# A transformer layer with compressive-memory attention and an MLP on one Trainium2 core: an opening written out in program order, first layer norms through ScalarE and a PSUM bank of their own, b2 added to the stored residual, late row blocks and first MLP weights placed anew

## The chip, the cores and the metric

One core of one Trainium2 chip runs the whole program. TensorE multiplies matrices into eight PSUM banks of 128 x 512 float32; VectorE (DVE), ScalarE (ACT) and GpSimd (POOL) do the elementwise work; SyncE (SP) issues most of the DMAs, in the order of its queue, and ScalarE issues some. Each engine runs its own instructions in order and waits for the others through semaphores. The metric is the device time of one execution in microseconds (us), lower is better; a kernel is timed in several runs, of which the median is given.

## The reference

S = 2048 rows of D = 1024, 32 heads of 32, four segments of 512 rows, and an MLP of width F = 3584, everything in float32:

```python
y = layernorm(x)
q, k, v = y @ wq, y @ wk, y @ wv
...
for s in range(4):
    a_dot = softmax(q_s k_s.T * 32 ** -0.5 + causal_mask) @ v_s
    a_mem = (phi(q_s) @ M) / (phi(q_s) @ z + 1e-6)
    o_s = g * a_mem + (1 - g) * a_dot
    M, z = M + phi(k_s).T @ v_s, z + sum(phi(k_s))
h = x + o @ wo
y2 = layernorm(layernorm(h))
out = h + gelu(y2 @ w1 + b1) @ w2 + b2
```

Here phi(t) is t + 1 above zero and exp(t) below, and g = sigmoid(beta), one number per head.

## The kernel before

*Numbers as two halves.* Every product of full precision is made of three fast ones: an operand is split into an upper half `h` (a rounded copy, on ACT or VectorE) and a lower half `l` (the operand minus `h`, on VectorE or POOL), and TensorE adds h·h, h·l and l·h into one bank (`mm3`, L110). `split` (L87) makes the two halves of a weight block, and `load_block` (L193) loads a 128-column block into one of the two `wr` buffers of the pool `wp` and splits it into `wh` and `wl` (three of each).

*Stages.* The rows are worked on in two halves of 1024, each of two segments of 512 (`sl` 0 and 1) or eight row blocks of 128.

- 0 to 22 us: the opening. The identity, the gates from beta and the transposed b1 are made (L53 to L75), and `ln1(0, 0)` (L181) normalises the first segment: it loads four row blocks `xt`, and for each `ln_scale` (L115) makes mean and scale (statistics on VectorE, the power on POOL), `ln_tiles` (L139) normalises, and `ln_transpose` (L127) transposes on TensorE into `pt`, copies the upper half on ACT (`yh`) and subtracts the lower half on VectorE (`yl`). In this one call the normalisation is an ACT instruction with scale and offset, the offset `nb` being made on VectorE.
- 22 to 575 us, and 930 to 1480 us for the second half: `attention`. `dense` makes q, k and v of four heads and one segment; each such unit is interleaved with the slots of the heads of the unit before. The first unit has no heads yet and is interleaved with `ln1(half, 1)`, the second segment's layer norm, instead.
- 530 to 648 and 1480 to 1558 us: `wo_seg`, the output projection. `finish` and its `fold` transpose a column block back and add it to the residual tiles `hts`. While the second segment goes through, `ln2` (L583) stores the first segment's finished residual to `h1_dram` (`store_h`, L579), normalises it in place and transposes it.
- 648 to 732 and 1558 to 1642 us: `Mixer.lead`, the first of the products of `w1`. The MLP's two multiplications are made by a Strassen scheme, that is by seven products of sums and differences of quarters instead of eight. `load`, `upper` and `lower` bring column blocks of `w1` (tiles `wx`, `wh`, `wl`). Beside it `ln2_combined` (L590) stores and normalises the second segment and forms the scheme's operands (`fold`, with tiles such as `b12t`).
- 732 to 930 and 1642 to 1841 us: `Mixer.pair`, twenty steps for one pair of column blocks, some 13.6 us each: products into `bps` and `dps`, GELU on ACT, results to `h_dram` in DRAM. Under the last nine pairs of the first half `ln1(1, 0, 2)` runs, a step of it for every 0.15 steps of the pairs.
- 1841 to 2393 us: `Second`, the product with `w2`, in 2 x 7 combinations of seven row blocks each (KP = 7). `load_rows` (L870) loads the rows of `w2` of one row block into a tile `w2r`, one of four buffers tagged "ln" in `lnp`; `fill` (L881) forms the combination (POOL), splits it (`hi` on ACT, `lo` on VectorE) and, for combinations 7 and 6, stores the sum to `t_dram` for later use, which holds the buffer until the store is done. `load_items` (L908) loads the rows of the hidden activations `hr` that the left operands are made of. `out` (L968) loads the stored residual into the tile `c`, to which `add` adds every product, and `bias` (L991) adds b2 to it in 32 steps after the eighth to the 43rd product. `fills` has a due time for every row block; `rows_ahead` (L902) loads as far ahead as four buffers allow, the b2 tile counted as one. Before the stage starts, `fill_at` (L1128) lists the places in the last pairs at which the first fourteen row blocks are filled; two of its combinations (q 0 and 1) have to be there when the stage starts.

*What sets the order.* Within `in_order()` (L98) each engine runs what is traced in program order; `lead`, the pairs and `Second` are traced inside it. Elsewhere, in the opening, the attention and the output projections, the scheduler of the language chooses the order from dependences; `queue_after` (L94) adds a single order between two instructions.

*PSUM.* Three banks have the tag "d" (`ps_dense`), two "qk", two "pt" and one "av". The transposes `pt` of the layer norms share the three "d" banks with `kps`, `qps`, `vps`, `pwo`, `pn`, `bps` and `dps`. The one "av" bank holds the attention's `po` of 64 partitions.

Of the kernel before, what the change touches and what calls it, by code (L numbers as in the profile page):

```python
# [16 lines left out]
P = 128  # L17
S = 2048
D = 1024
H = 32  # L20
# [22 lines left out]
def build(tc, x, wq, wk, wv, wo, beta, w1, b1, w2, b2, out):  # L43
# [20 lines left out]
    nc.sync.dma_start(bb, bass.AP(tensor=beta.tensor, offset=beta.offset, ap=[[0, P], [1, H]]))  # L64
    nc.scalar.activation(bb, bb, AF.Exp, scale=-1.0)
    nc.vector.tensor_scalar(bb, bb, 1.0, None, op0=ALU.add)
    nc.vector.reciprocal(gate[:, 0, :], bb)
    nc.vector.tensor_scalar(gate[:, 1, :], gate[:, 0, :], -1.0, 1.0, op0=ALU.mult, op1=ALU.add)

    b1r = const.tile([FB, P], F32, name="b1r")  # L70
    nc.sync.dma_start(b1r, b1.rearrange("(f p) -> f p", p=P))
    b1c = const.tile([P, FB], F32, name="b1c")
    pb = ps_dense("pb")
    nc.tensor.transpose(pb[:, :FB], b1r, ident[:FB, :FB])
    nc.vector.tensor_copy(b1c, pb[:, :FB])  # L75
# [11 lines left out]
    def split(pool, w, hi, lo, hi_eng="vector", lo_eng="gpsimd"):  # L87
        if hi_eng == "vector":
            acts["hi"] = nc.vector.tensor_copy(hi, w)
        else:  # L90
            acts["hi"] = nc.scalar.copy(hi, w)  # L91
        return getattr(nc, lo_eng).tensor_tensor(lo, w, raw(hi), op=ALU.subtract)  # L92

    def queue_after(late, early):  # L94
        tc.add_manual_dep(late.ins, early.ins.name, NOSYNC, reason="issue order")

    @contextmanager
    def in_order():  # L98
# [6 lines left out]
        for ins in traced[n:]:  # L105
            if ins.engine in last:
                tc.add_manual_dep(ins, last[ins.engine].name, NOSYNC, reason="program order")
            last[ins.engine] = ins

# [5 lines left out]
    def ln_scale(pool, src, double):  # L115
        st = pool.tile([P, 2, 6], F32, name="st", bufs=3)
        for i in range(2):
            nc.vector.bn_stats(st[:, i, :], src[:, 512 * i:512 * i + 512])
# [5 lines left out]
        acts["pow"] = nc.gpsimd.tensor_tensor(v[:, 1:2], v[:, 0:1], mhalf, op=ALU.pow)  # L124
        return mv[:, 0:1], v[:, 1:2]

    def ln_transpose(pool, src, xh, xl, t4):  # L127
        for c in range(2):
            pt = ps_dense("pt").rearrange("p (a b) -> p a b", a=4)
            for i in range(4):  # L130
# [6 lines left out]
                                    op=ALU.subtract)  # L137

    def ln_tiles(pool, tiles, xh, xl, double, gap=1, act=False, fold=None):  # L139
        fold = fold or (lambda src, t4: ln_transpose(pool, src, xh, xl, t4))  # L140
        for t in range(5):
            if t < 4:
                m, r = ln_scale(pool, tiles[t], double)
                for _ in range(gap):
                    yield
                if act:
                    nb = pool.tile([P, 1], F32, name="nb", bufs=4)
                    nc.vector.scalar_tensor_tensor(nb, m, -1.0, r, op0=ALU.mult, op1=ALU.mult)
# [32 lines left out]
    def ln1(half, sl, delay=0):  # L181
# [9 lines left out]
        yield from ln_tiles(lnp, xs, yh, yl, False, act=(half == 0 and sl == 0))  # L191

    def load_block(pool, w, c0, wbufs, hi_eng="vector", lo_eng="gpsimd"):  # L193
# [4 lines left out]
        acts["split"] = split(pool, wr, wh, wl, hi_eng, lo_eng)  # L198
        return wh, wl

    def attention(half):
# [3 lines left out]
        nc.gpsimd.memset(mask, 0.0)  # L205
# [4 lines left out]
        if half == 0:  # L210
            nc.gpsimd.memset(mz_flat, 0.0)
# [225 lines left out]
        def av(st, n):  # L437
            u, j = st["u"], st["j"]
            if n == 0:
                st["po"] = psum.tile([64, 512], F32, tag="av", name="po", bufs=1)  # L440
# [49 lines left out]
        def weights(g):  # L490
            ws = {}
            for n, w in (("k", wk), ("q", wq), ("v", wv)):
                ws[n] = load_block(wp, w, g * P, 3, "vector" if g or n == "k" else "scalar")
                if g == 0 and n != "k":
                    queue_after(acts["split"], acts["pow"])
            return ws

        ws = weights(0)
# [84 lines left out]
    def ln2(half, sl, hts):  # L583
# [3 lines left out]
        store_h(half, sl, hts)  # L587
        yield from ln_tiles(lnp, hts, zh, zl, True, 2)

    def ln2_combined(half, hts, zx):  # L590
# [9 lines left out]
        store_h(half, 1, hts)  # L600
# [44 lines left out]
        yield from ln_tiles(lnp, hts, None, None, True, 2, fold=fold)  # L645
# [533 lines left out]
```

## Time and profile before

| what | value |
| --- | --- |
| median of three runs | 2394.14 us (2392.71 to 2401.14) |
| profiled execution, its own time | 2394.96 us |
| span of its instructions | 2393.2 us |
| TensorE's mean granted clock | 0.993 |
| data moved by DMA | 356.95 MB, mean 149 GB/s |

How to read its lines: engines are PE (TensorE), DVE, ACT, POOL and SP, and L656 is line 656 of the kernel. In a timeline a row is start, duration, engine, line, operation, out<-in with shapes and, in brackets, how long the engine had stood idle and what released it. In the list of waits a row is the waiting instruction, what released it, total us, number of waits and the longest. In the groups, "x32 | 39.3, 1229 | 0.0" is 32 instructions, 39.3 us in all, 1229 ns each, and no idle time ahead of them. In the chain of waits a row is a step's start and duration. A window gives PE, PEld (weight loads), DVE, ACT and POOL busy time, with the number of instructions, then the granted clock, the share of the DMA engines and GB/s.

### The profile page before, as it was taken

Reading aid. Unit: us, or ns where it says so; the run is one execution under the profiler, and the core shown is the slowest. Engines: PE = TensorE matmul, PEld = TensorE weight load, DVE = VectorE, ACT = ScalarE, POOL = GpSimd, SP = SyncE. Lnnn points to the kernel's source line nnn. Section 1 sums busy time; section 2 is a strip of 40 time slices with the busy share of each in tenths; the row PEclk is TensorE's granted clock in tenths of the full one; section 3 lists DMA queues with packets and bytes.
Section 4 is the critical chain, followed back from the end, with each engine's and each line's share of the span. In section 5 each row is a group of like instructions: output and inputs, shape, how many; then the busy total and the mean of one; then the engine's idle time right before and its main releaser. Section 6 shows DMA issues by size and latency. Waiting matters only on the chain.

```text
span 2393.2 us, 35708 instructions
## 1 busy us (share of the span) xinstructions
PE 2308.3 (96%) x11873; PEld 1906.4 (80%) x11873; DVE 1628.4 (68%) x3470; ACT 1212.0 (51%) x2557; POOL 1065.5 (45%) x1011
## 2 busy tenths in 40 slices
PE   6999999999999989999999999999998989999999
PEld 5888888877787878888888877777886878888887
DVE  6777777775475664777777776466565888667763
ACT  4677676775363333677777776254343223232321
POOL 3444444444164442455555544245443554245430
PEclk9999999999999999999999999999999999999999
DMA  5333333333466654433333334366566976476762
GB/s 170 91 89 88 82 84 85 89 105 120 145 207 201 186 151 131 122 85 85 85 86 84 88 95 126 128 211 195 157 187 212 328 258 213 153 251 227 250 222 96
DMA packets 348161, 356.95 MB, mean 149 GB/s; under 512 B 26286, under 2 KB 251594, under 8 KB 347978
## 3 DMA queue, kind: packets, MB, share of 16 engines
q1 hardware_dynamic: 284810, 317.98, 44.3%
q10 hardware_dynamic: 63168, 36.71, 5.2%
q8 instruction: 94, 1.54, 0.3%
q14 instruction: 89, 0.73, 0.1%
HBM read 227.11 MB, written 77.14 MB: 127 GB/s over the span
## 4 chain that ended last, share of the span: by engine, by line
PE 72%; DVE 9%; ACT 6%; DMA 6%; issue 3%; POOL 3%; SPq 1%; ACTq 0%; DVEq 0%; POOLq 0%
PE po L1031 21%; PE bps L656 7%; PE ppt L428 5%; PE dps L656 5%; PE po L448 5%; PE pqk L396 3%; PE kps L111 2%; PE kps L112 2%; PE kps L113 2%; PE vps L111 2%; PE vps L112 2%; PE vps L113 2%; PE pwo L113 2%; PE pwo L111 2%; PE pwo L112 2%
## 5 line engine op out<-in xcount | busy, mean ns | idle before, releaser
L412 POOL TENSOR_SCALAR pr<-pr,nm,gate 128x128 f32<-128x128 f32 (+3 forms) x512 | 322.2, 639 | 409.0 <-DVE nm L409 307.3
L405 ACT ACTIVATE pr<-pr,mx 128x256 f32<-128x256 f32 (+3 forms) x512 | 287.8, 562 | 175.8 <-DVE mx L397 171.3
L397 DVE CUSTOM_DVE_ANT_0 pr<-pqk,mask 128x256 f32<-128x256 f32 (+3 forms) x512 | 243.4, 483 | 38.4 <-PE pqk L396 35.3
L435 DVE TENSOR_TENSOR ptl<-ppt,pth 128x512 fp32r<-128x512 f32 (+1 forms) x384 | 227.2, 597 | 53.5 <-ACT pth L430 51.4
L428 PE MATMUL ppt<-ident,pr 128*128 128x128 f32 x1280 | 222.7, 277 | 1.9 <-DVE ptl L435 1.8
L430 ACT CAST pth<-ppt 128x512 fp32r<-128x512 f32 (+1 forms) x384 | 194.1, 518 | 51.5 <-PE ppt L428 46.5
L92 POOL TENSOR_TENSOR wl<-wr,wh 128x1024 fp32r<-128x1024 f32 x64 | 152.9, 2390 | 103.2 <-ACT wh L91 48.4
L428 PEld LDWEIGHTS ppt<-ident,pr 128*128 128x128 f32 x1280 | 164.0, 140 | 32.1 <-DVE ptl L435 3.6
L1041 DVE TENSOR_TENSOR c<-c,po 128x512 f32<-128x512 f32 x160 | 105.2, 682 | 116.2 <-PE po L1031 115.8
L396 PE MATMUL pqk<-ks,qs 96*128 96x256 f32 (+3 forms) x512 | 162.7, 318 | 1.3 <-DVE mx L397 1.3
L448 PE MATMUL po<-ptl,vs 128*64 128x512 f32 (+3 forms) x512 | 154.2, 311 | 5.8 <-DVE ptl L435 5.6
L448 PE MATMUL po<-pth,vs 128*64 128x512 f32 (+3 forms) x512 | 155.5, 326 | 1.3 <-ACT pth L430 1.1
L888 POOL TENSOR_TENSOR w2r<-w2r 128x512 f32<-128x512 f32 x56 | 90.2, 1622 | 83.9 <-DMA w2r<-in_B_w 70.9
L1031 PE MATMUL po<-w2h,zh 128*128 128x512 f32 x378 | 122.2, 393 | 3.8 <-DVE zh L960 3.3
L409 DVE RECIPROCAL nm<-mx 128x2 f32<-128x2 f32 x256 | 42.2, 165 | 112.6 <-ACT pr L405 112.2
L396 PEld LDWEIGHTS pqk<-ks,qs 96*128 96x128 f32 x512 | 96.0, 188 | 26.4 <-DVE mx L397 6.3
L1031 PE MATMUL po<-w2h,hl 128*128 128x512 f32 x322 | 104.1, 393 | 6.4 <-DVE c L1041 6.4
L111 PE MATMUL vps<-yh,wh 128*128 128x512 f32 x256 | 109.0, 426 | 0.2 <-ACT omt L378 0.2
L111 PE MATMUL kps<-yh,wh 128*128 128x512 f32 x256 | 108.3, 423 | 0.0
L111 PE MATMUL qps<-yh,wh 128*128 128x512 f32 x256 | 107.2, 419 | 0.0
L111 PE MATMUL pwo<-oh,wh 128*128 128x512 f32 x256 | 104.8, 411 | 0.6 <-ACT oh L91 0.6
L113 PE MATMUL pwo<-oh,wl 128*128 128x512 f32 x256 | 101.5, 397 | 0.0
(233 smaller groups left out, 6751.5 us busy)
## 6 DMA issues: line engine op xcount, KB each, us to landing
hr<-h_dram SPq DMA_DIRECT2D x112, 448.0 KB, 5.0
w2r<-in_B_w SPq DMA_DIRECT2D x126, 256.0 KB, 3.9
r<-in_B_w SPq DMA_DIRECT2D x56, 512.0 KB, 4.5
h_dram<-ht ACTq DMA_DIRECT2D x84, 256.0 KB, 3.7
ks<-kh SPq DMA_DIRECT2D x256, 64.0 KB, 2.0
qs<-qh SPq DMA_DIRECT2D x256, 64.0 KB, 2.0
wr<-in_A_wo SPq DMA_DIRECT2D x32, 512.0 KB, 4.4
wx<-in_B_w SPq DMA_DIRECT2D x56, 256.0 KB, 3.6
```

The costliest lines, as they stand in the source:

```text
L111: nc.tensor.matmul(ps, ah, bh, start=first, stop=False)
L113: nc.tensor.matmul(ps, al, bh, start=False, stop=last)
L396: nc.tensor.matmul(pqk[:, :n], u["qs"][j][:, i * P:(i + 1) * P], u["ks"][j][:, 0:n], start=True, stop=True)
L397: nc.vector.tensor_tensor_reduce(out=st["pr"][:, offs[i]:offs[i] + n], in0=pqk[:, :n], in1=mask[:, 512 - n:512], op0=ALU.add, op1=ALU.min, ...
L405: nc.scalar.activation(pi, pi, AF.Exp, bias=mx[:, i:i + 1], scale=-1.0, accum_out=mx[:, 4 + i:5 + i])
L412: nc.gpsimd.tensor_scalar(pi, pi, nm[:, 4 + k:5 + k], gate[:, 1, 4 * g + j:4 * g + j + 1], op0=ALU.mult, op1=ALU.mult)
L428: nc.tensor.transpose(ppt[:, o:o + P], pr[:, offs[i] + jk * P:offs[i] + (jk + 1) * P], ident)
L430: nc.scalar.copy(pth[:, base:base + w], ppt[:, :w])
L435: nc.vector.tensor_tensor(o, x0, x1, op=ALU.subtract)
L448: nc.tensor.matmul(po[:, P * jk:], v, st[part][:, koff[jk]:koff[jk] + w], start=(jk, part) == (0, "pth"), stop=(jk, part) == (2, "ptl"))
L656: nc.tensor.matmul(ps, x_[:, c, :], y_[:, c, :], start=first and c == 0 and n == 0, stop=last and c == 3 and n == 2, skip_group_check=True)
L1031: nc.tensor.matmul(ps, x_[:, k], y_[k], start=opens and k == 0 and i == 0, stop=closes and k == self.KP - 1 and i == 2, skip_group_check=True)
```

## The change

- *Opening.* `opening()` takes the place of `ln1(0, 0)` and of the first `weights(0)`: all inside `in_order()`. SP loads the four blocks of x first, then the first blocks of wk and wq, then beta and b1 (the instructions on these are now in `constants()`, called late). Row blocks 0 and 3 are normalised on ACT, 1 and 2 on POOL; `nb` is made on POOL. The halves of wk, wq and wv are split at fixed places. `behind` puts the statistics of the following layer norm and three memsets of `attention` after the opening on their engines.
- *First layer norms.* `ln1` transposes into the "av" bank (`po` becomes the lower 64 partitions of a full tile) with one more step between its transposes, and normalises on ACT in every call (`act=True`), `nb` on POOL (`ln_offset`). Its rate beside the first unit of a half goes from 0.5 to 1.1 steps per step, and under the pairs from 0.15 to 0.16.
- *b2.* `ln2` loads b2 into a tile of the pool `pp`. For every row block, `residual` adds it on POOL into `hb` (two buffers) right after the block's statistics and stores `hb` instead of the tile itself. `store_h` and `Second.bias` are removed, and with them the b2 tile in the ring of four.
- *Late row blocks.* Row blocks 4 and 5 of combination 1 are loaded into the `wr` buffers of `wp` (`APART`), and the last eight places of `fill_at` are moved.
- *First MLP weights.* The loads of w1's blocks -1 and 0 and the split of -1 move from `lead` into `begin`, called at the 57th step of the second `wo_seg`.

```diff
+    def constants():
+        nc.scalar.activation(bb, bb, AF.Exp, scale=-1.0)
...
+    def behind(op):
+        tc.add_manual_dep(op.ins, acts["last"][op.ins.engine].name, NOSYNC, reason="program order")
...
-            nc.vector.bn_stats(st[:, i, :], src[:, 512 * i:512 * i + 512])
+            op = nc.vector.bn_stats(st[:, i, :], src[:, 512 * i:512 * i + 512])
+            if "last" in acts:
+                behind(op)
...
+    def ln_offset(pool, m, r):
+        nb = pool.tile([P, 1], F32, name="nb", bufs=4)
+        nc.gpsimd.tensor_scalar(nb, m, -1.0, r, op0=ALU.mult, op1=ALU.mult)
+        return nb
...
-            pt = ps_dense("pt").rearrange("p (a b) -> p a b", a=4)
+            pt = (take or ps_dense)("pt").rearrange("p (a b) -> p a b", a=4)
...
+            if take:
+                yield
...
+                if act:
+                    nb = ln_offset(pool, m, r)
+                if aside:
+                    aside(t)
...
-                    nb = pool.tile([P, 1], F32, name="nb", bufs=4)
-                    nc.vector.scalar_tensor_tensor(nb, m, -1.0, r, op0=ALU.mult, op1=ALU.mult)
...
-        yield from ln_tiles(lnp, xs, yh, yl, False, act=(half == 0 and sl == 0))
+        def take(name):
+            return psum.tile([P, 512], F32, tag="av", name=name, bufs=1)
+
+        yield from ln_tiles(lnp, xs, yh, yl, False, act=True,
+                            fold=lambda src, t4: ln_transpose(lnp, src, yh, yl, t4, take))
+
+    def opening():
...
+        with in_order():
+            scale(0)
+            scale(1)
+            normal(0)
+            normal(1)
+            scale(2)
+            normal(2)
+            turn(0)
+            lower(0, 0)
+            scale(3)
+            turn(1)
+            halves("k", "vector")
+            lower(1, 0)
+            turn(2)
+            normal(3)
+            lower(2, 0)
+            turn(3)
+            lower(3, 0)
+            lower(3, 1)
+            halves("q", "scalar")
+            load("v", wv)
+            constants()
+            halves("v", "scalar")
+        return ws
...
-                    interleave(d, ln1(half, 1), 0.5)
+                    interleave(d, ln1(half, 1), 1.1)
...
-    def store_h(half, sl, hts):
-        for t in range(4):
-            nc.sync.dma_start(h1_dram[half * NT + 4 * sl + t], hts[t])
...
+        def aside(t):
+            hb = pp.tile([P, D], F32, name="hb", bufs=2)
+            nc.gpsimd.tensor_tensor(hb, hts[t], b2c, op=ALU.add)
+            nc.sync.dma_start(h1_dram[half * NT + 4 * sl + t], hb)
...
+            load(-1)
+            load(0)
+            upper(-1)
+            lower(-1)
+            self.early = load, upper, lower, left
...
+        APART = ((1, 4), (1, 5))
...
+            if (q, k) in self.APART:
+                t = wp.tile([P, DC, P], F32, tag="wr", name="w2s", bufs=2).rearrange("p a b -> p (a b)")
...
-                    len(self.rows) + (self.b2c is not None) < 4:
+                    (len(self.rows) - sum(r in self.rows for r in self.APART) < 4):
...
-            if n > 6 and self.b2c is not None and n % 16 < 14:
-                t, c = self.unbiased.pop(0)
-                o = self.out(t, c)
-                nc.vector.tensor_tensor(o, o, self.b2c[:, c * 512:(c + 1) * 512], op=ALU.add)
...
-        interleave(wo_seg(half, 1, hts1, pp, iter(()), evac), ln2(half, 0, hts), 0.5)
+        interleave(hooked(wo_seg(half, 1, hts1, pp, iter(()), evac), lambda k: mixer.begin(), 57, 1),
+                   ln2(half, 0, hts, pp), 0.5)
...
-            interleave(chain(*(mixer.pair(j) for j in range(HP - 9, HP))), ln1(1, 0, 2), 0.15)
+            interleave(chain(*(mixer.pair(j) for j in range(HP - 9, HP))), ln1(1, 0, 2), 0.16)
...
-            fill_at = [(j, 5) for j in range(HP - 8, HP - 2)] + [(HP - 3, 13), (HP - 2, 12), (HP - 2, 14), (HP - 1, 0),
-                       (HP - 1, 2), (HP - 1, 4), (HP - 1, 6), (HP - 1, 9)]
+            fill_at = [(j, 5) for j in range(HP - 8, HP - 2)] + [(HP - 3, 13), (HP - 2, 12), (HP - 2, 15), (HP - 2, 18),
+                       (HP - 1, 1), (HP - 1, 5), (HP - 1, 9), (HP - 1, 13)]
```

More of the change, by code (lines that the diff above doesn't have):

```diff
@@ L599, in ln2_combined @@
         B = acts["B"]
-        store_h(half, 1, hts)
         sub = ALU.subtract
@@ L643, in fold @@
             halves("T4", t4s, nc.gpsimd)
-        yield from ln_tiles(lnp, hts, None, None, True, 2, fold=fold)
+        yield from ln_tiles(lnp, hts, None, None, True, 2, fold=fold, aside=residual(half, 1, hts, pp))
     HP = FB // 2
@@ L1058, in zx_tile @@
         return acts["zx"].tile([P, 4, 512], F32R, tag=f"t{x_}{n}", name=f"z{x_}{n}")
-    for _ in ln1(0, 0):
-        pass
+    first = opening()
     for half in range(2):
-        rest = attention(half)
+        rest = attention(half, None if half else first)
         hts = [lnp.tile([P, D], F32, tag="ln", name="ht0", bufs=4) for _ in range(4)]
```

128 lines of the change are left out of this document (82 added, 46 removed).

## The prediction

> **What bounds it now.** I read the page first, then the list of TensorE's waits, then the timeline at each long wait.
>
> ```profile
> span 2393.2 us, 35708 instructions
> PE 2308.3 (96%) x11873; PEld 1906.4 (80%) x11873; DVE 1628.4 (68%) x3470; ACT 1212.0 (51%) x2557; POOL 1065.5 (45%) x1011
> ```
>
> TensorE is the bound, and the change takes no matmul away. What can be won lies in the stretches in which TensorE stands still. The longest entries of its waits (waiter, releaser, total us, times, longest):
>
> ```profile
> PE pt L132 <- ACT xt L149: 7.2, 1, 7.2
> PE pt L132 <- DVE yl L136: 6.7, 4, 3.4
> PE po L1031 <- DVE c L1041: 6.4, 1, 6.4
> PE bps L656 <- DVE u L796: 5.7, 1, 5.7
> PE pt L132 <- DVE ht L565: 3.7, 2, 2.7
> PE bps L656 <- DVE yl L136: 3.6, 1, 3.6
> PE pt L132 <- DVE kl L283: 3.4, 1, 3.4
> PE po L1031 <- DVE zh L960: 3.3, 1, 3.3
> PE cps L656 <- ACT wh L701: 2.5, 2, 1.2
> PE pt L132 <- DVE mv L120: 1.3, 1, 1.3
> ```
>
> Each entry is a single place or two, and nearly each belongs to a part of the change. A long wait costs more than itself, as the matmuls behind the 3.4 us wait show (start, duration):
>
> ```profile
> 36.84 0.63 PE L113 MATMUL qps<-yh,wl 128*128 128x512 f32 x1
> 37.26 0.63 PE L111 MATMUL qps<-yh,wh 128*128 128x512 f32 x1
> 39.48 0.39 PE L112 MATMUL qps<-yl,wh 128*128 128x512 f32 x1
> 39.71 0.40 PE L113 MATMUL qps<-yh,wl 128*128 128x512 f32 x1
> ```
>
> They start 0.42 us apart instead of 0.23, for some 3 us. I price this at 1.5 us after each wait of over 2.3 us (estimate: 3 us at about half rate). The Trainium skill (TensorE: Matmul & The Clock Gate, "Part 1: The HAM clock gate") says that about 3.4 us of idleness halves the array's clock and as long a busy stretch restores it; the rows agree. By that rule the new opening, in which TensorE idles between row blocks, might start the first projection at half rate, and the sum would be 1.5 us higher.
>
> **(a) Opening and first projections.**
>
> ```profile
> 0.72 0.39 SPq L64 DMA_DIRECT2D bb<-in_A_beta  x1
> 1.66 1.78 SPq L186 DMA_DIRECT2D xt<-in_A_x  x4
> L148 DVE SCALAR_TENSOR_TENSOR nb<-mv,v x4: 158/160/2287, 10.0 to 14.7; 128x1 f32<-128x1 f32 x4
> 14.64 2.34 POOL L92 TENSOR_TENSOR wl<-wr,wh 128x1024 fp32r<-128x1024 f32 x1
> 22.73 0.50 PE L112 MATMUL kps<-yl,wh 128*128 128x512 f32 x1 [0.16 <-DVE yl L136]
> 49.52 0.47 PE L111 MATMUL kps<-yh,wh 128*128 128x512 f32 x1
> L412 POOL TENSOR_SCALAR pr<-pr,nm,gate 128x512 f32<-128x512 f32 x128 | 99.9, 781 | 0.0
> ```
>
> Moving x ahead of beta and b1 on SP's queue starts it at 0.72 instead of 1.66: -0.9. The fourth `nb` on VectorE took 2.29 us instead of 0.16 because POOL's 2.34 us subtraction started 0.06 us before it; with nb on POOL this 2.1 us goes. Against them: two normalisations move to POOL, where the nearest row is the same operation on half the columns, 0.78 us (so 0.8 to 1.6 us each, and I take 1.6), and the second of them holds up the statistics of block 3, whose normalisation also stands behind block 2's copies on ACT. I put back 0.5: -2.5, between 0 and -4. POOL's wk subtraction, now behind the row statistics, is covered by the transposes of blocks 2 and 3.
>
> From 22.73 to 49.52 are 26.8 us, of which 72 matmuls (three projections of eight chunks, three products each) need 72 x 0.23 = 16.6. The wait for `kl` (3.4, and 1.5 slow) came because the second segment's transposes took banks from the three that the projections use. In the bank of `po`, idle until the first attention product, this wait has no cause. But now eight transposes, copies and subtractions use one bank in turn, all within the first unit, on an ACT that also normalises. I put back 2 of the 4.9: -2.9, between 0 and -4.9. ACT's queue then holds projection copies behind a late normalisation. Together **a = -5.4**. In the second half the same edit meets no long wait: 0, within 1.5 either way.
>
> **(b) Layer norm under the half-0 pairs.** Its transposes leave the three banks of the MLP products, its normalisations leave VectorE for ACT, and `nb` goes to POOL.
>
> ```profile
> 843.69 0.71 PE L132 MATMUL pt<-ident,xt 128*128 128x128 f32 x4 [2.37 <-DVE yl L136]
> ```
>
> The waits that go are 2.4 here, the 3.6 of `bps` on `yl`, and 1.3 on `mv`: 7.3, with two slow restarts 10.3. VectorE also sheds its share, a normalisation per block with the wait for `v` before it. With an extra yield the bank has a whole side step to be freed. ACT's extra normalisation is hidden beside TensorE; what could come late next is the GELU or an operand's upper half. I take **b = -9**, between -5 and -10.3.
>
> **(c) Late row blocks.** The rows of `w2` come through a ring of four buffers, each held until its sum was stored. In the chain of waits, SP's timeline, and the DVE groups:
>
> ```profile
> 1821.84 4.93 DMA t_dram<-w2r
> 1831.26 8.50 DMA t_dram<-w2r
> 1840.20 3.49 DMA w2r<-in_B_w
> 1827.69 3.48 SPq L918 DMA_DIRECT2D hr<-h_dram  x6
> 1936.64 2.56 DVE c L999
> L999 DVE TENSOR_TENSOR c<-c,b2c 128x512 f32<-128x512 f32 x32 | 39.3, 1229 | 0.0
> ```
>
> Row blocks 4 and 5 wait for a store each, and block 6 for a store that sat behind six loads of `hr`. VectorE, in program order, then holds the adds for which `bps` (5.7) and `po` (3.3) wait. Two rows in the idle `wr` buffers can be loaded without these stores; block 6 then needs only the first buffer to be freed, and its load stands ahead of the `hr` loads. A load takes 3.5 us and the last four conversions are spread over the last pair, so all should be in time. What is late next is `hr`, now queued behind three rows' loads: 1 us left. The waits are 9.0, with two restarts 12: **c = -11**, between 0 and -12.
>
> **(d) b2 out of the last stage.** 32 adds, 39.3 us of VectorE, and one ring buffer, held until they end. The 6.4 us wait comes at 1933 to 1940, where three free buffers serve seven rows and a b2 add of 2.56 us stands just ahead of the add awaited. With four buffers a row is loaded one fill earlier. Value 6.4 + 1.5 = 7.9; I take **d = -6.5**, between 0 and -7.9. The other b2 adds lie beside a TensorE that doesn't wait.
>
> **(e) First MLP weights ahead.** `begin` loads and splits block -1 one column block before the lead. Its buffers are those of `wo` blocks already consumed; ACT and VectorE are mostly idle there. It takes away the 2.5 us of `cps` on `wh`: **e = -2.4**, between 0 and -2.5. If a `wo` split came late it would wait in the same queues.
>
> **(f) b2 added on POOL, in the lead.** Sixteen adds of 128x1024, in both layer norms of each half. Nearest rows, on POOL and on VectorE:
>
> ```profile
> L92 POOL TENSOR_TENSOR wl<-wr,wh 128x1024 fp32r<-128x1024 f32 x64 | 152.9, 2390 | 103.2 <-ACT wh L91 48.4 <-DVE wh L89 31.8 <-PE pqk L396 16.3
> L92 DVE TENSOR_TENSOR wl<-wr,wh 128x1024 fp32r<-128x1024 f32 x16 | 19.6, 1223 | 18.1 <-ACT wh L91 18.1
> ```
>
> So 2.4 us each. In the lead POOL is not idle. The window gives PE, PEld, DVE, ACT and POOL busy time; the rest is the chain of waits:
>
> ```profile
> 674.30:718.20 43.90, 43.48 (x204) 35.63 (x203) 39.29 (x39) 29.23 (x46) 35.55 (x24) 1.00 0.53 157
> 659.43 5.45 DMA h_dram<-ht
> 664.90 7.70 DMA wx<-in_B_w
> 674.31 1.85 POOL b12t L627
> 684.95 0.56 POOL v L124
> 686.27 2.32 DVE wl L707
> 717.10 3.67 DMA wx<-in_B_w
> ```
>
> Over 43.9 us POOL is busy for 35.6 and VectorE for 39.3, they pass work back and forth, and a VectorE split takes 2.32 instead of 1.22 us when POOL runs beside it. Four folds and the statistics of blocks 2 and 3 lie there, so two adds come in, 4.8 us, right on the chain between `v` and `b12t`. For it: four 512 KB stores no longer stand at once ahead of `wx` (5.45 and 7.70 us, after which POOL's chain starts) nor ahead of block 0's normalisation. I count 3 back. SP now waits for an add before each store, with the next `wx` loads behind it. I take +2 per half, **f = +4**, between -6 and 8 x 2.4 = +19.
>
> **(g) b2 beside the output projection.** The normalisation, in place, waited for its store:
>
> ```profile
> 609.87 0.81 DVE L151 TENSOR_SCALAR ht<-ht,mv,v 128x1024 f32<-128x1024 f32 x1 [8.21 <-DMA h_dram<-ht]
> ```
>
> Behind it on VectorE stood the residual adds for which the transposes wait (3.7 over both halves). Now it waits for an add, which waits for the b2 load, put where the first store was on SP's queue. If that load lands as late, the normalisation is 2.4 us later, 4.8 in all; if the residual adds are issued first, the 3.7 and a restart vanish, -5.2. The order is not written out there. Nearest is the queue place of the row above: **g = +4**, between -5 and +8.
>
> **Sum.** -5.4 - 9 - 11 - 6.5 - 2.4 + 4 + 4 = -26.3. The profiled execution took 2394.96 us, 0.8 above the median of 2394.14: 2368.7, as a median **2368**.
>
> **Rivals.**
>
> *The rows stay late.* The two `wr` buffers serve the last pair's weights too; freed late, their loads block SP and with it the `hr` loads. For it: SP's queue is in order and already blocked here. Against: these weights are combined a pair earlier. c and d give nothing: 2368 + 17.5 = 2385.5.
>
> *One bank is too few.* Transposes stand in TensorE's queue until VectorE has freed the bank, so the wait moves from `bps` to `pt`. For it: the subtraction was the releaser of these waits. Against: it has a whole side step now. It takes back 2.9 of a and 9 of b: 2380.
>
> *POOL becomes the bound (slower).* All sixteen adds, where normalisations, folds and stores wait for them, come on the path, each doubling a VectorE pass: 16 x (2.4 + 1.1) = 56 in place of the 8 of f and g: 2416. It decides from 26.3 + 8 = 34 us, 2.1 us an add. For it: the lead's chain already runs through POOL; against: only four adds fall into its crowded part, and beside the output projection POOL mostly idles. The Trainium skill (GPSIMD Engine Reference, "4.1 Engine selection") speaks for this rival: it gives elementwise adds to VectorE, as about twice as slow on GpSimd, and "8. Key points" adds that the two contend for SBUF interfaces. The two rows of f agree.
>
> **Chances.** The forecast 67% (its own range 2356 to 2378), late rows 10%, one bank 10%, POOL 7%, and 6% for a gain beyond the forecast's range. The range 2354 to 2388 holds the forecast and the first two rivals and leaves out POOL and the far tail. Less than 0.5% (12 us) can't be told from no change here: faster is below 2382, the forecast, the far gain and half of "one bank", 78%; no change 15%; slower 7%.
>
> **What would show it.** a: first projection matmul near 20 instead of 22.7, the second unit's near 44. b: no `pt` or `bps` wait on `yl` under the pairs. c, d: no wait on `u`, `zh` or `c` over 1 us around the last stage's start and one seventh into it. e: no `cps` wait on `wh`. f: POOL's window fuller, waits of `cps` on `wl` grown by some 2 us. g: `pt` waiting on residual adds for over 2 us. The prediction fails if waits reappear under other names where these stood, or if the adds lengthen the leads by more than 10 us.

## The result and the profile after

The changed kernel takes 2398.95 us (median of 12 runs, 2393.84 to 2402.93) against 2397.73 of the kernel before in the same comparison (12 runs): ratio 1.0004, 95% interval 0.9993 to 1.0016. That is no change, 31 us above the forecast of 2368 and 11 above its range. The profiled execution took 2397.52 us, 2.6 more than the one of before. On its page:

```profile
span 2395.7 us, 35706 instructions
PE 2309.7 (96%) x11873; PEld 1909.5 (80%) x11873; DVE 1586.2 (66%) x3422; ACT 1224.1 (51%) x2567; POOL 1111.9 (46%) x1043
```

VectorE lost 42 us of work and POOL gained 46; TensorE is still the bound, at 96%. Its waits, in the form shown for before:

```profile
PE pt L140 <- DVE ht L658: 13.2, 2, 6.6
PE pt L250 <- ACT xt L240: 10.5, 2, 8.7
PE cps L756 <- ACT p L825: 10.4, 7, 2.5
PE po L1131 <- DVE c L1141: 6.3, 2, 3.7
PE pt L250 <- POOL xt L242: 4.9, 2, 3.2
PE pt L140 <- ACT xt L161: 4.7, 2, 2.8
```

All waits under the pairs (`pt` and `bps` on `yl`, `pt` on `mv`) and both of `cps` on `wh` are gone, and some 27 us of others came: `pt` on the residual adds `ht` (13.2 for 3.7), `cps` on the copies `p` (10.4 for 2.1), `pt` on POOL's `xt` (4.9), and `pt` on ACT's `xt` beside the first units (L161, 4.7). The row of 10.5 us on L240 is not new: most of it is the start of the program, 8.7 us, in which TensorE has nothing to do yet. To see what each part gave, the two traces are cut where a stage's first matmul starts. The cuts of the kernel after, then those of the kernel before:

```profile
23.82 0.79 PE L112 MATMUL kps<-yh,wh 128*128 128x512 f32 x1 [0.31 <-DVE yl L259]
595.98 0.39 PE L112 MATMUL pwo<-oh,wh 128*128 128x512 f32 x1
656.18 0.39 PE L756 MATMUL cps<-zh,wh 128*128 128x512 f32 x1
745.43 0.39 PE L756 MATMUL bps<-th,sa 128*128 128x512 f32 x1
935.51 0.39 PE L112 MATMUL kps<-yh,wh 128*128 128x512 f32 x1
```

```profile
594.91 0.39 PE L111 MATMUL pwo<-oh,wh 128*128 128x512 f32 x1
648.77 0.50 PE L656 MATMUL cps<-zh,wh 128*128 128x512 f32 x1 [1.25 <-ACT wh L701]
732.07 0.39 PE L656 MATMUL bps<-th,sa 128*128 128x512 f32 x1
933.20 0.39 PE L111 MATMUL kps<-yh,wh 128*128 128x512 f32 x1
```

The lead, from the first `cps` to the first `bps`, is 745.43 - 656.18 = 89.25 long, and was 83.30. The second half's cuts were taken in the same way. Stage lengths in us:

| stage | term | forecast | before | after | difference |
| --- | --- | --- | --- | --- | --- |
| opening, to the first projection matmul | a | -2.5 | 22.10 | 23.82 | +1.7 |
| first unit, half 0 | a | -2.9 | 27.41 | 27.09 | -0.3 |
| rest of the attention, half 0 | - | 0 | 545.40 | 545.07 | -0.3 |
| output projection, second segment, half 0 | g, e | +0.8 | 53.86 | 60.20 | +6.3 |
| lead, half 0 | f | +2 | 83.30 | 89.25 | +6.0 |
| pairs, half 0 | b | -9 | 201.13 | 190.08 | -11.1 |
| attention, half 1 | a | 0 | 568.44 | 571.74 | +3.3 |
| output projection, second segment, half 1 | g, e | +0.8 | 57.12 | 60.26 | +3.1 |
| lead, half 1 | f | +2 | 82.96 | 89.20 | +6.2 |
| pairs, half 1, and the first eight products | c | -11 | 244.02 | 237.09 | -6.9 |
| all later products | d | -6.5 | 507.44 | 501.94 | -5.5 |

The savings came: b, c, d and e (1.4 us in each output projection's last column block) are 26 us. The two places where b2 is now added took 24 of them back, and a, meant to give 5.4, cost 4.7.

Each column is one profiled execution. The profiles of the experiments below show how much a stage varies where its code is the same as in the changed kernel: the pairs of half 0 take 190.0 to 191.7 us, the stretch of c 236.3 to 240.1, that of d 500.8 to 507.3. So b and c are well outside this spread; against the 507.4 of before, d's saving lies anywhere between nothing and 6.6.

### The profile page after: what moved, and what is told of

The parts are those of the page before. It is cut to its first block, busy times and chain, and to the rows that moved or that the text cites. A ratio compares the mean times of both kernels' runs of the same rounds, so it can differ in the third digit from the quotient of the medians.

```text
span 2395.7 us, 35706 instructions
## 1 busy us (share of the span) xinstructions
PE 2309.7 (96%) x11873; PEld 1909.5 (80%) x11873; DVE 1586.2 (66%) x3422; ACT 1224.1 (51%) x2567; POOL 1111.9 (46%) x1043
## 4 chain that ended last, share of the span: by engine, by line
PE 74%; DVE 8%; ACT 6%; DMA 5%; POOL 3%; issue 3%; SPq 1%; ACTq 0%; DVEq 0%; POOLq 0%
PE po L1131 21%; PE bps L756 8%; PE dps L756 5%; PE ppt L522 5%; PE po L542 5%; PE pqk L490 3%; PE kps L112 2%; PE kps L114 2%; PE kps L113 2%; PE vps L112 2%; PE vps L113 2%; PE vps L114 2%; PE qps L113 2%; PE qps L112 2%; PE qps L114 2%
## 5 line engine op out<-in xcount | busy, mean ns | idle before, releaser
L524 ACT CAST pth<-ppt 128x512 fp32r<-128x512 f32 (+1 forms) x384 | 194.2, 518 | 53.7 <-PE ppt L522 46.8
L1001 POOL TENSOR_TENSOR w2r<-w2r 128x512 f32<-128x512 f32 x54 | 84.7, 1581 | 61.1 <-DMA w2r<-in_B_w 43.0
L113 PE MATMUL qps<-yl,wh 128*128 128x512 f32 x256 | 102.3, 400 | 0.0
```

The lines of the kernel that those rows point to most:

```text
L113: nc.tensor.matmul(ps, ah, bl, start=False, stop=False)
L524: nc.scalar.copy(pth[:, base:base + w], ppt[:, :w])
```

## The experiments

The kernels' stage lengths below are cut in the same way; ratios are to the kernel before, with 95% intervals.

### What makes the b2 part dear

In the changed kernel's first lead, row block 1 (timelines of POOL, VectorE, SP, ACT and TensorE):

```profile
692.21 2.40 POOL L678 TENSOR_TENSOR hb<-ht,b2c 128x1024 f32<-128x1024 f32 x1
694.65 1.76 DVE L163 TENSOR_SCALAR ht<-ht,mv,v 128x1024 f32<-128x1024 f32 x1 [3.09 <-POOL hb L678]
694.64 0.34 SPq L679 DMA_DIRECT2D h_dram<-hb  x1
695.15 1.60 SPq L792 DMA_DIRECT2D wx<-in_B_w  x2
700.90 1.05 ACT L800 CAST wh<-wx 128x1024 fp32r<-128x1024 f32 x1 [6.09 <-DMA wx<-in_B_w]
703.41 0.57 ACT L825 COPY p<-cps 128x512 f32<-128x512 f32 x1
704.04 0.50 PE L756 MATMUL cps<-zh,wh 128*128 128x512 f32 x1 [1.79 <-ACT p L825]
```

Two waits for the add end at 694.6: the normalisation, which overwrites `ht` in place, has waited 3.1 us; and SP's queue, which stood at the store, goes on to the load of `wx`, for which ACT then waits 6.1 us with the copy `p` behind it. In the output projection there is a third: the load of b2, issued at 603.31, lands at 610.9.

```profile
610.96 2.53 POOL L678 TENSOR_TENSOR hb<-ht,b2c 128x1024 f32<-128x1024 f32 x1 [0.80 <-DMA b2c<-in_B_b]
613.53 5.62 DVE L163 TENSOR_SCALAR ht<-ht,mv,v 128x1024 f32<-128x1024 f32 x2 [2.29 <-POOL hb L678]
619.07 0.28 DVE L658 TENSOR_TENSOR ht<-pn,ht 128x128 f32<-128x128 f32 x1
620.00 0.48 PE L140 MATMUL pt<-ident,ht 128*128 128x128 f32 x1 [6.61 <-DVE ht L658]
```

Which of the three counts? `late_store` issues each store one block later:

```diff
+            if held:
+                nc.sync.dma_start(*held.pop())
...
-            nc.sync.dma_start(h1_dram[half * NT + 4 * sl + t], hb)
+            held.append((h1_dram[half * NT + 4 * sl + t], hb))
```

> Each store of a sum with b2 is issued one row block later on SP's queue; nothing else moves. Theory Q (the queue): SP stands at the store until POOL's add is done, the w1 loads behind it are late, and ACT, waiting 6 us for them, holds up the copies that the first products wait for. Then the leads (first cps matmul to first bps matmul) shrink from 89.2 us each to about 84 to 85.5, and the kernel gets 8 to 10 us faster (ratio to the kernel before about 0.997). Rival P (the adds' own time): POOL's 2.4 us add and the slower VectorE pass behind it make the loss; then the leads stay at 88 to 89 us and the time does not move.

Measured: 2404.97 us, ratio 1.0029 (1.0016 to 1.0042), leads 90.4 and 89.7. The queue was freed, and nothing was won:

```profile
698.19 1.06 ACT L807 CAST wh<-wx 128x1024 fp32r<-128x1024 f32 x1 [0.85 <-DMA wx<-in_B_w]
697.21 1.76 DVE L163 TENSOR_SCALAR ht<-ht,mv,v 128x1024 f32<-128x1024 f32 x1 [3.08 <-POOL hb L685]
714.75 0.30 PE L722 MATMUL pt<-ident,ht 128*128 128x128 f32 x1 [1.83 <-DVE ht L163]
```

ACT's wait for `wx` fell from 6.1 to 0.9, but the normalisation waits as before and TensorE now waits for it. Theory Q fell. `early_b2` loads b2 ahead of x:

```diff
         hts1 = [pp.tile([P, D], F32, name=f"ht1{i}") for i in range(4)]
+        acts["b2"] = pp.tile([P, D], F32, name="b2c")
+        nc.sync.dma_start(acts["b2"], ...)
         load_x(half, 1, hts1)
```

> The load of b2 is issued ahead of the four loads of x instead of behind them; nothing else moves. Theory L (the late load): the first add starts only when b2 has landed, the normalisations wait for the adds, and the residual adds behind them on VectorE make TensorE wait 6.6 us in each half. Then that wait falls below 2 us, the second segment's output projection (its first pwo matmul to the first cps matmul) shrinks from 60.2 to 53 to 56 us in each half, and the kernel gets 9 to 13 us faster. Rival P: the adds on POOL and the normalisations slowed beside them hold VectorE wherever they stand; then the wait stays above 5 us and the time moves by less than 3 us.

Measured: 2401.37 us, ratio 1.0011 (1.0000 to 1.0023), output projections 60.1 and 60.8. The wait for the residual adds fell from 13.2 to 2.5 us, and one of `pwo` on `zl` (a bank not yet freed) came, 9.5 us in two places; VectorE stands still for POOL's adds, now earlier and again at the third block:

```profile
607.19 2.88 DVE L163 TENSOR_SCALAR ht<-ht,mv,v 128x1024 f32<-128x1024 f32 x1 [4.30 <-POOL hb L678]
617.24 2.81 DVE L163 TENSOR_SCALAR ht<-ht,mv,v 128x1024 f32<-128x1024 f32 x1 [3.52 <-POOL hb L678]
```

`no_b2` prices the part by leaving it out: the tiles are stored as they are, and b2 is added nowhere.

```diff
-            hb = pp.tile([P, D], F32, name="hb", bufs=2)
-            nc.gpsimd.tensor_tensor(hb, hts[t], b2c, op=ALU.add)
-            nc.sync.dma_start(h1_dram[half * NT + 4 * sl + t], hb)
+            if t == 0:
+                for k in range(4):
+                    nc.sync.dma_start(h1_dram[half * NT + 4 * sl + k], hts[k])
```

> Leaves out the addition of b2: the residual tiles are stored themselves as before the change, with no load of b2 and no add. It prices the b2 part of the change alone. If all of the loss in the output projections and the leads belongs to it: output projections 52 to 56 us, leads 83 to 84 us, and about 24 us faster, near 2374 us. If the early weight blocks or the smaller number of steps beside them share in it: 2382 us or more, with leads or output projections still 3 us above those of the kernel before.

Measured: 2379.73 us, ratio 0.9931 (0.9909 to 0.9953); output projections 54.6 and 55.8, leads 84.5 and 86.4. That lies between the two expectations. So some 19 us belong to b2, and 1 to 3.5 us of each lead do not (or come from stores placed otherwise; that was left open). `both_b2` makes both edits of the first two at once, the adds still on POOL:

> The load of b2 ahead of the loads of x and each store of a sum one row block later, the adds on POOL as in the changed kernel. If the late load and the blocked queue cover for each other: leads 84 to 86 us, output projections 55 to 57, some 15 us faster. If the add on POOL is itself the price: leads 88 us or more, output projections 59 or more, time within 5 us of the changed kernel's 2399.

Measured: 2404.04 us, ratio 1.0028 (1.0010 to 1.0047), leads 90.4 and 89.5, output projections 60.9 and 60.0. The two transfers don't cover for each other. `add_dve` moves the add alone:

```diff
-            nc.gpsimd.tensor_tensor(hb, hts[t], b2c, op=ALU.add)
+            nc.vector.tensor_tensor(hb, hts[t], b2c, op=ALU.add)
```

> The sixteen adds of b2 go from POOL to VectorE; stores and loads keep their places. Two runs left the loss where it was when the store or the load of b2 was moved, so the add itself, between statistics and normalisation, is now the first theory (P): 2.4 us on POOL and a normalisation slowed to 1.8 to 2.9 us behind it. Then with 1.2 us on VectorE, no change of engine and no slowed pass, the leads fall from 89.2 to 84 to 86 us and the output projections from 60.2 to 55 to 57, 14 to 18 us in all. Rival D: VectorE, busy for 39 of 44 us in the lead, can't take them: leads stay at 88 us or more.

Measured: 2378.44 us, ratio 0.9924 (0.9910 to 0.9937), output projections 54.9 and 54.8, leads 86.0 and 83.3. One word is worth some 20 us, and with the adds on VectorE the kernel takes no longer than without any (2379.73). The groups of the normalisation and of the add (min/median/max ns), after, then with `add_dve`:

```profile
L678 POOL TENSOR_TENSOR hb<-ht,b2c x16: 2334/2399/2675, 611.0 to 1620.0; 128x1024 f32<-128x1024 f32 x16
L163 DVE TENSOR_SCALAR ht<-ht,mv,v x16: 800/2016/2886, 613.5 to 1622.5; 128x1024 f32<-128x1024 f32 x16
  POOL hb L678: 23.6, 8
```

```profile
L678 DVE TENSOR_TENSOR hb<-ht,b2c x16: 1166/1184/3404, 610.9 to 1601.0; 128x1024 f32<-128x1024 f32 x16
L163 DVE TENSOR_SCALAR ht<-ht,mv,v x16: 801/811/1778, 613.2 to 1602.9; 128x1024 f32<-128x1024 f32 x16
```

On POOL a block costs 2.4 + 2.0 us, one behind the other, and VectorE idles 23.6 us for the adds; on VectorE 1.2 + 0.8, though that engine is the busier one. Rival D fell. Three things go together in this edit: the wait for the add, the slower normalisation behind it, and POOL's own time. What each is worth alone was not tried. The Trainium skill (GPSIMD Engine Reference, "4.1 Engine selection") gives such adds to VectorE, and these runs agree.

### The opening

POOL's two normalisations, in the changed kernel and with `open_muladd`, which multiplies and adds instead of subtracting and multiplying:

```profile
8.48 3.79 POOL L242 TENSOR_SCALAR xt<-xt,mv,v 128x1024 f32<-128x1024 f32 x1
13.29 4.17 POOL L242 TENSOR_SCALAR xt<-xt,mv,v 128x1024 f32<-128x1024 f32 x1
```

```profile
8.89 1.20 POOL L241 TENSOR_SCALAR xt<-xt,v,nb 128x1024 f32<-128x1024 f32 x1
11.47 1.20 POOL L241 TENSOR_SCALAR xt<-xt,v,nb 128x1024 f32<-128x1024 f32 x1
19.50 0.79 PE L112 MATMUL kps<-yh,wh 128*128 128x512 f32 x1 [0.31 <-DVE yl L258]
```

`open_dve` came first:

```diff
-                nc.gpsimd.tensor_scalar(xs[t], xs[t], m, r, op0=ALU.subtract, op1=ALU.mult)
+                nc.vector.tensor_scalar(xs[t], xs[t], m, r, op0=ALU.subtract, op1=ALU.mult)
```

> In the opening, row blocks 1 and 2 are normalised on VectorE instead of POOL. Theory N (POOL's normalisations of 3.8 and 4.2 us set the opening's end): the first projection matmul comes at 18.5 to 20.5 us instead of 23.8, 3 to 5 us off the total. Rival V: VectorE, in program order with the statistics and the subtractions, takes over the chain: 22 us or later, and less than 2 us off the total.

Measured: 2396.85 us, ratio 0.9998 (0.9988 to 1.0008); the first projection matmul at 21.61. Between the two theories: a normalisation takes 0.81 us there, but VectorE does statistics, normalisations and subtractions in turn. `open_muladd` and `open_halves` keep POOL. Each ran once, so their starts are read and not their times:

```diff
-                nc.gpsimd.tensor_scalar(xs[t], xs[t], m, r, op0=ALU.subtract, op1=ALU.mult)
+                nc.gpsimd.tensor_scalar(xs[t], xs[t], r, scales[t][2], op0=ALU.mult, op1=ALU.add)
```

> In the opening POOL normalises row blocks 1 and 2 as x times r plus nb (multiply and add) instead of x minus m, times r; two more small instructions make nb. If the operation subtract is what takes 3.8 to 4.2 us, each takes about 1.6 us (twice the 0.78 of the nearest row) and the first projection matmul comes near 20.5 us. If it is the width or the engine: still 3.5 us or more and 23.8 or later.

> In the opening POOL normalises row blocks 1 and 2 in two instructions of 128x512 each instead of one of 128x1024. If width makes it slow: 0.8 us each and the first projection matmul near 20.5 us. If it goes by elements: 1.9 us each and 23.8 us.

`open_muladd` starts at 19.50 (2392.36 us); `open_halves`, two instructions of 512 columns, still takes 4.15 us for a block and starts at 23.42 (2396.95 us).

```profile
8.32 4.15 POOL L244 TENSOR_SCALAR xt<-xt,mv,v 128x512 f32<-128x512 f32 x2
```

So the width is not what makes it slow. The operation is the likely cause; the operand `mv`, which gave way to `nb` in the same edit, was not changed alone.

### Beside the first units

Three edits of the second segment's layer norm: its pace 0.75 (`slow_side`), its normalisation back on VectorE (`vec_side`, `act=sl == 0`), and a slow start (`late_start`, pace 0.7, then 1.5).

> Beside the first unit of each half the layer norm runs at 0.75 steps per step instead of 1.1, which is the pace per row block of before (six steps for four). Theory E (too early): the transposes stand in TensorE's queue before ACT has normalised; with a slower pace the waits of pt on xt (3.0 at 34 us, 2.0 at 949 us) end, and the first units shrink from 27.1 and 30.0 us to 25 and 28, some 4 us in all. Rival A: ACT's normalisation, behind nb on POOL and the weights' subtractions there, is late at any pace: less than 1 us.

> The second segment's first layer norm, beside the first unit of each half, is normalised on VectorE as before the change, without nb; its transposes keep the av bank and the pace of 1.1. Theory A (nb on POOL and ACT's normalisation make xt late): the waits of pt on xt end, first units 27.1 and 30.0 us shrink to 25 and 28. Rival T (the statistics are late: VectorE's behind the opening's last instructions, the powers on POOL behind the weights' subtractions): pt now waits for VectorE's xt about as long, and the first units change by less than 1 us.

> Beside the first unit the layer norm starts slowly (0.7 steps per step over ten steps) and then catches up (1.5), so that its first transposes stand later in TensorE's queue and its last ones not at the end. If the wait of pt on xt is only a matter of the first transposes' place, it falls from 3.0 and 2.0 us below 1, and the first units shrink from 27.1 and 30.0 us to 25 and 28.5. If the catching up crowds the one av bank, pt waits for yl instead and nothing is won.

`slow_side`: 2401.59 us, ratio 1.0025 (1.0011 to 1.0038), first units 30.0 and 31.6; theory E fell. The waits of `pt` on `xt` stay at 4.7 us together, as rival A said, and the last transposes now stand one behind the other at the unit's end, where they wait for `yl` (up to 1.2 us). `vec_side`: 2398.02, ratio 0.9997 (0.9986 to 1.0008), 26.7 and 28.9. `late_start`: 2397.76, 0.9996 (0.9985 to 1.0007), 26.9 and 29.3. Neither of the last two differs from the changed kernel beyond the intervals, and a unit varies by 1.5 us without any edit. `vec_side`'s wait has another name and most of its length, as theory T said, here in the changed kernel and then there:

```profile
34.29 0.48 PE L140 MATMUL pt<-ident,xt 128*128 128x128 f32 x1 [2.85 <-ACT xt L161]
```

```profile
33.54 0.33 PE L140 MATMUL pt<-ident,xt 128*128 128x128 f32 x1 [2.23 <-DVE xt L163]
```

Two rows of `hr_first`, which is the same up to here, set against the changed kernel (the wait, then a window of 4 us behind it; the number before the last two is the granted clock):

```profile
948.62 0.33 PE L140 MATMUL pt<-ident,xt 128*128 128x128 f32 x1 [1.87 <-ACT xt L161]
949.00:953.00 4.00, 4.00 (x15) 3.19 (x14) 0.69 (x1) 3.68 (x5) 2.34 (x8) 0.58 0.64 220
```

```profile
948.30 0.66 PE L140 MATMUL pt<-ident,xt 128*128 128x128 f32 x4 [1.87 <-ACT xt L161]
949.00:953.00 4.00, 4.00 (x21) 3.23 (x20) 1.02 (x3) 3.97 (x7) 2.27 (x8) 1.00 0.55 187
```

Behind the same wait of 1.87 us the clock is halved in one run (15 matmuls in 4 us) and not in the other (21). The first units of the two halves take 27.1 and 30.0 us in the one, 25.6 and 28.4 in the other: 1.5 us each is the restart. In sixteen profiles the code of the second half's first unit is the same, and the wait is 1.87 to 1.89 us in each; behind it the clock was halved in six, where the unit takes 30.0 us, and not in ten, where it takes 28.4 to 29.0. Without the restart a gave 1.8 us in the first unit and lost 0.6 in the second half's.

The list of waits doesn't show that the first projection itself now starts slowly, as the prediction thought possible. Its third and fourth matmul before, then its second and third after, where the first is at 23.82:

```profile
23.07 0.40 PE L113 MATMUL kps<-yh,wl 128*128 128x512 f32 x1
23.30 0.39 PE L111 MATMUL kps<-yh,wh 128*128 128x512 f32 x1
```

```profile
24.41 0.63 PE L113 MATMUL kps<-yl,wh 128*128 128x512 f32 x1
24.84 0.63 PE L114 MATMUL kps<-yh,wl 128*128 128x512 f32 x1
```

Before, the matmuls soon stand 0.23 us apart; after, the first eight gaps are 0.43 us or more, 1.7 us lost in all. But the unit did not end later for it: in `hr_first` twelve gaps are slow, and yet `pt`, which waits for ACT's `xt`, comes 10.45 us after the first matmul, as against 10.47 here. The wait (1.91 us there, 2.85 here) took up the loss.

### The late row blocks and the fastest versions

`no_apart` (`APART = ()`) sends all rows through the ring again:

> All rows of w2 go through the ring of four buffers again; the new places of the fills and everything else stay. Theory R (the two extra buffers carry the gain at the start of the last stage): the last pairs and the first seventh of it, 1790 to 1894 us, become 5 to 9 us longer, with waits of bps or po on late subtractions. Rival F (the new places of the fills carry it): less than 2 us longer.

Measured: 2406.90 us, ratio 1.0041 (1.0027 to 1.0055); pairs of half 1 and the first eight products 246.0 us instead of 237.1. The two extra buffers carry the gain. What may have kept c from its 11 us is in the changed kernel's SP and TensorE rows:

```profile
1825.95 9.66 SPq L991 DMA_DIRECT2D w2s<-in_B_w  x4
1837.81 0.48 SPq L1031 DMA_DIRECT2D hr<-h_dram  x1
1863.56 0.59 PE L1131 MATMUL po<-zh,zl 128*128 128x512 f32 x1 [3.69 <-DVE c L1141]
```

The rows' loads stand 9.7 us on SP's queue for the `wr` buffers, ahead of the `hr` loads. `hr_first` holds them back until those are issued:

> The loads of the two late row blocks wait on SP's queue until the first activations' loads have been issued. Theory H (the rows' loads, blocked 9.7 us for their buffers, make the activations late, and VectorE's splits of them stand ahead of the adds that po waits for): the 3.9 us wait of po on c at 1864 falls below 1.5, 3 to 5 us off. Rival L (the rows are then too late themselves): their splits come in the last pair's end, a wait of bps or po on them appears, and the time stays or grows by up to 5 us.

```profile
1852.14 0.76 PE L756 MATMUL bps<-zh,sb 128*128 128x512 f32 x1 [10.48 <-DVE u L906]
1869.70 0.47 PE L1132 MATMUL po<-zh,zl 128*128 128x512 f32 x1 [0.88 <-DVE c L1142]
```

Rival L holds: the rows, now late, make `bps` wait 10.5 us. The wait of 3.7 falls to 0.9, as theory H said, but TensorE has just stood still for 10.5 us, in which everything else could catch up; so this run doesn't show that the late `hr` loads made the wait. In sum 2405.28 us, ratio 1.0032 (1.0019 to 1.0045).

`late_bias` stores the tiles without b2, adds b2 in the last stage from the 21st product on, and has `open_dve`; `later_bias` starts at the 27th, with `open_muladd`. `best` is `add_dve` with `open_dve`, `best_early` adds `early_b2`, `best_muladd` is `add_dve` with `open_muladd`.

> A version meant to be fast: the tiles are stored without b2; b2 is added in the last stage as before the change, but from the 21st product on instead of the 8th; the opening normalises row blocks 1 and 2 on VectorE. If the other parts of the change are worth what the stages show: leads 84 to 87 us, output projections 54 to 56, no wait of TensorE over 1 us while b2 is added, 2375 to 2380 us (ratio 0.992). If adding b2 in the last stage costs the 6.4 us wait wherever it stands: 2382 to 2387.

> The tiles are stored without b2, b2 is added in the last stage from the 27th product on, and the opening normalises with multiply and add. If it was the place (beside the 21st product, where the rows of the next combination are filled) that cost late_bias 2.6 us: the 8 products from the 17th on take 40 to 41 us instead of 43.6, and the time is 2371 to 2375. If the adds or the buffer that b2 holds cost it anywhere: another wait of po appears further on and the time is 2376 or more.

> The two edits that paid, together: b2 added on VectorE, and row blocks 1 and 2 of the opening normalised on VectorE. If they are independent: 20.5 and 3.2 us less than the changed kernel's 2399, so 2374 to 2377 us, ratio 0.991; leads 83 to 86 us, output projections 55, first projection matmul at 21.6. If the earlier start is lost again further on: 2378 or more.

> As best, and the load of b2 ahead of the loads of x. With the add on POOL this order changed nothing, since POOL's adds took VectorE's time wherever they stood. With the add on VectorE the load is now what VectorE stands still for (8.5 us, until 610 us). Theory: the 4.0 us of pt waiting for residual adds in both halves go, with a restart or two, so 3 to 6 us off best's 2376.4, 2370 to 2374. Rival: the normalisations and adds then meet the other work as they did with early_b2, another wait takes the place, and the time stays within 2 us of best.

> b2 added on VectorE in both layer norms, and POOL's normalisations in the opening as multiply and add. If the two are independent: first projection matmul at 19.5 us, leads 83 to 86, output projections 55, and 4 us less than add_dve's 2378: 2373 to 2376, ratio 0.990. If the earlier start is lost again, as part of it was in best: 2377 or more.

| kernel | us | ratio, interval | leads | output projections |
| --- | --- | --- | --- | --- |
| `late_bias` | 2379.34 | 0.9931, 0.9918 to 0.9945 | 84.1, 84.8 | 53.5, 53.0 |
| `later_bias` | 2375.10 | 0.9900, 0.9882 to 0.9917 | 84.7, 87.9 | 53.0, 52.8 |
| `best` | 2376.40 | 0.9915, 0.9901 to 0.9929 | 85.7, 83.3 | 54.9, 54.6 |
| `best_early` | 2378.25 | 0.9913, 0.9893 to 0.9933 | 87.1, 86.1 | 53.7, 54.2 |
| `best_muladd` | 2374.19 | 0.9893, 0.9872 to 0.9914 | 85.5, 84.6 | 55.0, 54.6 |

`best` and `best_muladd` came out as expected for edits that are independent. In `later_bias` the eight products from the 17th on take 40.5 us instead of 43.6, as expected if the place counts. That doesn't confirm it: in kernels whose last stage is that of the changed kernel, with no b2 add in it at all, the same eight products take 39.5 (`best_muladd`) to 45.7 us (`slow_side`). `best_early` won 1.3 and 0.4 us in the output projections and lost 1.4 and 2.8 in the leads: its theory fell. `best_muladd` beats both kernels by some 25 us; between it and the next ones the intervals overlap.

## Why the prediction was wrong

From the forecast of -26.3 to the +2.6 of the two profiled executions are 29 us. f and g make 16.5 of them, a 10 and c and d 5; b and e gave 2.5 back.

- *f failed, and with it the forecast.* The step said "+2 per half": two adds come in, "right on the chain between `v` and `b12t`", less 3 us for the stores. The chain was named rightly and then mis-sized: 6.0 and 6.2 us. What was left out is the normalisation behind the add, 2.0 instead of 0.8 us. Of the 3 us counted back for the stores nothing shows: with `add_dve`, whose stores are spread in the same way, the leads are 86.0 and 83.3, not below the 83.3 and 83.0 of before. The store ahead of `wx` did block SP, as the step said; but freeing it (`late_store`) gives nothing, since the normalisation is as late. The wait that grew is `cps` on `p`, not on `wl`.
- *g failed*: +4 with the end at +8; it was +12.3 (7.8 and 4.6, output projections less the 1.4 of e). The late load was foreseen as the cause; it is not (`early_b2`, `both_b2`). Each normalisation waits for an add and then runs beside the next one, and the residual adds stand behind both.
- *a failed in its first half.* The nearest row, half the columns at 0.78 us, was taken for the same operation, but it multiplies twice (L412): 3.8 and 4.2 instead of 1.6. (The first projection matmul of before is at 22.10; the prediction took the second, at 22.73, for it.) POOL's subtraction of wk, "covered by the transposes", then came behind them. The first unit gave 0.3 of its 2.9, and a restart took 1.5 of the rest. In the second half the edit was to cost 0, within 1.5; it cost 3.3, of which a restart is 1.6. The first projection at half rate, for which the prediction would have added 1.5, came, but a wait took it up.
- *b was right*, 11.1 for 9 with the end at 10.3: all waits on `yl` and `mv` went, and none came, so one bank was not too few.
- *c and d were right in kind, too large*: 6.9 for 11 and 5.5 for 6.5, the latter uncertain by its spread. "In time" was wrong for the rows' loads, which is the first rival in part: the `wr` buffers came free late. `hr`, named as late next with 1 us, was issued 10 us later than before (1837.81 for 1827.69), and a wait of 3.7 stands behind it; that the one caused the other is not shown. Of d's wait 2.6 us are left, without any b2 add beside it:

```profile
1944.16 0.47 PE L1131 MATMUL po<-w2h,hl 128*128 128x512 f32 x1 [2.60 <-DVE c L1141]
```

- *e was right*: 2.8 for 2.4.
- *The slower rival* had the mechanism: adds ahead of normalisations, each slowing a VectorE pass. Its price of 56 was twice the 24 measured, and it was given 7%, because POOL was looked at for free time and not for what waits behind it. With the opening's miss and the smaller c it was enough to cancel all the savings.

## What to carry to other kernels

An operation put on an engine with time to spare still costs its full length where the next operation of its chain, here a normalisation in place, waits for it; and a slower engine beside VectorE also lengthens that next operation. Before pricing a queue or a load as the cause of a wait, ask what comes last once it is gone: two transfers looked late here, and moving them won nothing. And a duration is carried over only between rows of the same operation.

## What was not expected of the hardware

POOL's two-scalar pass over 128x1024 took 1.20 us as multiply and add, and 3.79 to 4.17 as subtract and multiply; two halves of it took 4.15. On VectorE the second form takes 0.81. Which of its two operations makes it slow on POOL, or whether an operand does, was not tried.

The clock after a wait is not set by its length alone: 1.87 us at one place led to 0.58 in one run and 1.00 in another. The Trainium skill (TensorE: Matmul & The Clock Gate, "Part 1: The HAM clock gate") says that the window in which activity is measured runs free, and that the time of a transition depends on where in it the first matmul lands. These rows agree that more than the length counts. The Trainium skill puts the halving after at least one idle window of about 3.4 us; here 1.87 us was enough, and the measurement decides.
